# A fused attention and mixture-of-experts kernel: the routing's small tables and one product move from SBUF to PSUM

## The chip, the cores and the metric

The kernel runs on one core of a Trainium2 chip. The metric is device time in microseconds of one execution. A time is the median of several runs; beside it stands one execution recorded by the hardware profiler, from which every row below is taken.

The core has TensorE (PE, matrix products into PSUM; PEld is its weight load), VectorE (DVE), ScalarE (ACT), GpSimd (POOL) and SyncE (SP, which here issues DMAs). [...]

## What is computed

The reference has three stages: a causal attention with a cumulative bias, a mixture of eight experts with a capacity of 288 tokens each, and a gated feed-forward layer. Cut to the two stages that the change is in:

```
logits = x @ w_gate                      # x: attention's output, 2304 tokens x 512
order = argsort(-logits.flatten())       # greedy: best (token, expert) pairs first
for idx in order:
    tok, e = idx // 8, idx % 8
    if assigned[tok] >= 0 or counts[e] >= 288: continue
    assigned[tok] = e; counts[e] += 1
for e in range(8):
    mask = assigned == e
    out[mask] = relu(x[mask] @ w1[e]) @ w2[e]        # first layer, 1024 wide
h = out @ w_in                           # second layer, 2048 wide
g = h * tanh(softplus(h))
return g @ w_out
```

All data are float32 at the interface, some weights of the second layer arrive as 64-bit floats.

## The kernel before

Attention runs first (0 to about 295 us) and leaves x in DRAM and the gate's logits in `L`, 128 partitions x 18 x 8. Then `experts` handles one expert at a time; each takes the 288 tokens of its set through both layers.

**Products in three parts.** Every float32 operand of a large product is split into a high and a low part, and `mm3` (L446) issues three matmuls, high by high (L448), high by low (L449), low by high (L450). ScalarE writes the high part, then VectorE or GpSimd the low part as a difference. The splits of the first layer's weights are on ScalarE (L417) and GpSimd (L418, two SBUF inputs, 128x512), in four rotating buffers `wt`; those of the second layer's weights, done once, on ScalarE (L83) and GpSimd (L84), after three integer steps on VectorE (L101, L104, L107) that turn 64-bit floats into 32-bit ones. The function `conv` inserts these steps one at a time between other work from the first routing until the end of expert 0.

**`up(e)`** is the first layer: for each of 8 slices m a group of 12 matmuls into a bank `hp` (pool `ps_h`, three banks), `act` from it (ScalarE L507, VectorE L508), and one slice later 12 matmuls from `act` into four banks `y`. **`down(e)`** is the second: for each of 16 slices f a group of 12 matmuls into an `hp` bank, `mish` on it, and three slices later (LAG) 12 matmuls `y` from the result.

**`mish(f, p, gs)`** computes the activation of bank `p`. VectorE copies `min(p, 20)` to an SBUF buffer `a` (printed as `c`, L541), ScalarE applies four functions to `a` in place (L542 to L545), then `product` (L548, VectorE) multiplies `a - 0.5` by `p` into `a`, ScalarE writes the high part from `a` (L550), and `low` (L554, VectorE) the low part from `a` and the high part. `product` is issued four ticks after `mish` and `low` one tick later; the matmuls of a slice contain four ticks. L548 is the last reader of the bank `p`.

**`route(e)`** finds the tokens of the next expert that is to be handled. It is a generator that yields how many steps of the main work are to be issued before it goes on. Expert 0's routing runs alone with the conversion (the first routing, 295 to 350 us); the routing for expert e+1 is issued in pieces between the matmuls of `up(e)` and `down(e)`. It computes each token's best logit `m` and its expert `oh` (L246, L248), then makes six searches for a threshold. `search` (L251) compares `m` with T candidates (`mask`, L253, 128 x 18 x T; T is 64 in the first two searches, 32 in the others), counts by 18 small matmuls (L258), flags (L262), spreads the result by a diagonal matrix `diag` (L264) and a matmul (L266), and reduces it to `J` (L269). Between searches, L278 to L308 make the next candidates (`k2`, `x2`, `th2`, `b2`, `cx`, `th`, `field`). After that L310 to L357 pick the expert and count places, L360 builds one-hot slots in three instructions, and L365 to L372 the token indices, with which GpSimd gathers rows (L377). The last routing (for expert 7) has no search. The small results lie in SBUF; the matmuls of the routing write a bank of `ps_r`, a new tile each time (`rbank`, L238).

**Order.** The instructions of an engine run in the order in which the Python code issues them; an instruction that waits holds up all that are behind it on its engine. VectorE's queue thus mixes the routing, L508, L541, L548 and L554, and, until the end of expert 0, the conversion.

Of the kernel before, what the change touches and what calls it, by code (L numbers as in the profile page):

```python
# [23 lines left out]
CAP = N // E  # L24
# [3 lines left out]
def fb(ap):  # L28
    return ap.bitcast(F32)
# [181 lines left out]
def experts(ctx, tc, K, ring, ident, L, x_dram, w1, w2, cv, out):  # L211
# [26 lines left out]
    def rbank():  # L238
        return ps_r.tile([128, 512], F32, name="rt")

    def small(shape, dt, name, bufs=2):
        return rot.tile(shape, dt, name=name, bufs=bufs)

    def route(e):
        m = small([128, NT], F32, "m")
# [5 lines left out]
        def search(th, T, lead):  # L251
# [4 lines left out]
            p = rbank()  # L256
# [7 lines left out]
            nc.vector.tensor_scalar(diag[:E], ident[:E, :E], n, None, op0=OP.mult)  # L264
# [3 lines left out]
            J = small([128, 1], F32, "J")  # L268
# [6 lines left out]
        else:  # L275
# [3 lines left out]
            k2 = small([128, 64], I32, "k2", 1)  # L279
# [6 lines left out]
            b2 = small([128, 1], I32, "b2")  # L286
# [5 lines left out]
            for T, step, jr in steps:  # L292
                th = small([128, 32], I32, "th", 1)
                if field is None:
                    nc.vector.tensor_copy(th[:, :T], jr)
                else:
                    nc.vector.tensor_scalar(th[:, :T], jr, field, None, op0=OP.add)
                nc.vector.tensor_tensor(th[:, :T], th[:, :T], cx.to_broadcast([128, T]), op=OP.bitwise_xor)
                yield from search(th[:, :T], T, 6 if side["up"] else 8)
                nf = small([128, 1], F32, "field")  # L300
                if field is None:
                    nc.vector.tensor_scalar(nf, R["J"], step, None, op0=OP.mult)
                else:
                    nc.vector.scalar_tensor_tensor(nf, R["J"], step, field, op0=OP.mult, op1=OP.add)
                field = nf
            li = small([128, 1], I32, "li")
            nc.vector.tensor_copy(li, field)
            nc.vector.tensor_tensor(li, li, cx, op=OP.bitwise_xor)  # L308
            lam = fb(li)
        ge = small([128, NT], BF16, "ge")  # L310
# [4 lines left out]
        p = rbank()  # L315
        nc.tensor.matmul(p[:, 0:8 * NT], onesF, geoh.rearrange("p c e -> p (c e)"), start=True, stop=True)
        yield 4
        cnt = small([128, E], F32, "cnt")
# [4 lines left out]
        se = small([128, E], F32, "se")  # L323
# [11 lines left out]
        nc.vector.tensor_sub(g2[:, NT:], sel, fb(g2)[:, 0:NT])  # L335
        yield 8
        p = rbank()
# [6 lines left out]
        sl = small([128, 2 * NT], F32, "sl", 1)  # L344
        nc.vector.tensor_add(sl, p[:, 64:64 + 2 * NT], cb)
        nc.vector.scalar_tensor_tensor(sl, fb(g2), -4096.0, sl, op0=OP.mult, op1=OP.add)
        slf = small([128, NT], F32, "slf")
        nc.vector.tensor_tensor(slf, sl[:, 0:NT], sl[:, NT:], op=OP.min)
        jg = small([128, NT, 2], F32, "jg", 1)
        for j in range(2):  # L350
            nc.vector.tensor_scalar(jg[:, :, j], slf, JW * (j + 1) - 0.5, None, op0=OP.is_ge)
        sr = small([128, NT], F32, "sr", 1)
        nc.vector.scalar_tensor_tensor(sr, jg[:, :, 0], -float(JW), slf, op0=OP.mult, op1=OP.add)
        nc.vector.scalar_tensor_tensor(sr, jg[:, :, 1], -float(JW), sr, op0=OP.mult, op1=OP.add)
# [8 lines left out]
        p = rbank()  # L363
# [5 lines left out]
        idf = small([128, NJ + 1], F32, "idf")  # L369
        nc.vector.memset(idf[:JW, NJ:], 0.0)  # L370
        nc.vector.tensor_reduce(idf[:JW, 0:NJ], p[:JW, 0:2 * NJ].rearrange("p (j k) -> p j k", k=2), axis=AX.X, op=OP.add)
        nc.vector.tensor_sub(idx[:JW], idf[:JW, 0:NJ], idf[:JW, 1:])  # L372
# [8 lines left out]
        if e + 1 < E:  # L381
            pt = small([128, NT], F32, "pt")
            nc.vector.tensor_scalar(pt, slf, CAP - 0.5, NEG, op0=OP.is_lt, op1=OP.mult)
            pe = small([128, E], F32, "pe")
# [153 lines left out]
    def mish(f, p, gs):  # L538
# [8 lines left out]
        def product():  # L547
            nc.vector.scalar_tensor_tensor(a, a, 0.5, p[:, :CAP], op0=OP.subtract, op1=OP.mult)  # L548
            g = ring("act", [128, 2, CAP], F32R)
            nc.scalar.activation(g[:, 0], a, AF.Copy, scale=-2.0)  # L550
            later(1, low, g)

        def low(g):
            nc.vector.scalar_tensor_tensor(g[:, 1], a, -2.0, fb(g)[:, 0], op0=OP.mult, op1=OP.subtract)  # L554
            gs[f] = g
# [575 lines left out]
```

## Time and profile before

| | us |
|---|---|
| median of 3 runs | 1113.09 (1109.98 to 1115.66) |
| the profiled execution, as timed | 1109.15 |
| its span, first to last instruction | 1107.4 |
| TensorE busy | 977.1 (88%) |
| VectorE busy | 751.0 (68%) |
| ScalarE busy | 631.4 (57%) |
| GpSimd busy | 442.5 (40%) |
| mean granted clock of TensorE | 0.933 of full speed |

The profile's page gives the busy time of each engine, the groups of instructions, and the chain of work that ended last. A query of the trace lists instructions in order of time, groups them by line and shape, gives for a line the shortest, median and longest duration, lists which engine waited for which, or gives busy times and the granted TensorE clock of a stretch. "L253" is line 253 of the kernel, and `mask<-m,th` names output and inputs of an instruction; `c` is the buffer `a` of `mish`, `rt` the bank of the routing.

### The profile page before, as it was taken

What the parts mean: (1) busy time and instruction counts of PE and PEld (TensorE: products, weight loads), DVE (VectorE), ACT (ScalarE), POOL (GpSimd) and SP (SyncE); (2) the same over time, 40 slices, a digit from 0 to 9 for tenths busy, and PEclk for the clock granted to TensorE, in tenths of its full rate; (3) what the DMA queues carried; (4) which work ended last, traced back from release to release, by engine and by line L of the source; (5) the groups of instructions that cost most, each with busy time, mean ns of one, the idle gap of its engine ahead of it and who ended that gap; (6) DMA issues with size and microseconds to landing.
All of it is one profiled execution on the core that took longest, in us unless ns stands there. A gap on an engine that the chain in (4) does not pass through costs nothing.

```text
span 1107.4 us, 21467 instructions
## 1 busy us (share of the span) xinstructions
PE 977.1 (88%) x7625; PEld 932.6 (84%) x7625; DVE 751.0 (68%) x2024; ACT 631.4 (57%) x1405; POOL 442.5 (40%) x441
## 2 busy tenths in 40 slices
PE   6899999999514799979989997997998899899996
PEld 5788888888513788879979997997998899899996
DVE  7768788887797889766566656656666575744243
ACT  5567775777622356626735652762574466376574
POOL 5555665666575623450241043026025103700601
PEclk8889997999855899999999999998999999999998
DMA  5898899782325424230330121123023012500300
GB/s 131 180 212 190 196 208 202 184 193 61 99 77 164 143 68 126 78 90 1 98 98 2 55 87 56 39 60 98 2 82 97 19 39 77 150 21 13 97 1 22
DMA packets 134579, 105.58 MB, mean 95 GB/s; under 512 B 63976, under 2 KB 114312, under 8 KB 134440
## 3 DMA queue, kind: packets, MB, share of 16 engines
q1 hardware_dynamic: 122520, 83.50, 30.5%
q10 hardware_dynamic: 8880, 11.27, 3.4%
q0 software_dynamic: 3072, 9.44, 2.7%
q8 instruction: 60, 0.98, 0.4%
q14 instruction: 47, 0.39, 0.1%
HBM read 69.55 MB, written 9.73 MB: 72 GB/s over the span
## 4 chain that ended last, share of the span: by engine, by line
PE 53%; DVE 23%; issue 11%; DMA 4%; POOL 4%; ACT 4%; SPq 1%; ACTq 0%; POOLq 0%; DVEq 0%
PE hp L448 7%; PE y L449 7%; PE y L448 6%; PE y L450 6%; PE hp L450 6%; PE hp L449 6%; DVE mask L253 4%; PE pv L969 2%; POOL wt L418 2%; PE rt L258 2%; PE pv L971 1%; PE t L863 1%; PE s L931 1%; PE pv L970 1%; DMA qkraw<-in_k_dram 1%
## 5 line engine op out<-in xcount | busy, mean ns | idle before, releaser
L418 POOL TENSOR_TENSOR wt<-raw,wt 128x512 fp32r<-128x512 f32 x128 | 166.1, 1312 | 399.7 <-ACT wt L417 386.4
L948 POOL TENSOR_TENSOR Pl<-P,Ph 128x384 fp32r<-128x384 f32 (+2 forms) x128 | 137.0, 1077 | 98.0 <-DVE Ph L947 44.0
L448 PE MATMUL hp<-xu,WI 128*128 128x288 f32 x512 | 153.5, 300 | 6.2 <-DVE c L548 6.2
L448 PE MATMUL y<-act,WO 128*128 128x288 f32 x512 | 156.5, 306 | 0.0
L449 PE MATMUL y<-act,WO 128*128 128x288 f32 x512 | 152.2, 297 | 1.7 <-DVE act L554 1.5
L450 PE MATMUL y<-act,WO 128*128 128x288 f32 x512 | 151.9, 297 | 0.0
L450 PE MATMUL hp<-xu,WI 128*128 128x288 f32 x512 | 151.7, 296 | 0.0
L449 PE MATMUL hp<-xu,WI 128*128 128x288 f32 x512 | 149.9, 293 | 0.9 <-DVE xu L526 0.9
L417 ACT ACTIVATE wt<-raw 128x512 fp32r<-128x512 f32 x128 | 79.6, 624 | 74.5 <-PE y L450 41.1
L548 DVE SCALAR_TENSOR_TENSOR c<-c,hp 128x288 f32<-128x288 f32 x128 | 57.8, 452 | 81.3 <-ACT c L545 81.3
L449 PE MATMUL y<-act,wt 128*128 128x288 f32 x256 | 81.0, 316 | 27.3 <-DVE act L508 27.3
L448 PEld LDWEIGHTS hp<-xu,WI 128*128 128x128 f32 x512 | 96.4, 188 | 7.8 <-DVE c L548 7.8
L449 PEld LDWEIGHTS y<-act,WO 128*128 128x128 f32 x512 | 97.0, 189 | 2.3 <-DVE act L554 2.3
L449 PEld LDWEIGHTS hp<-xu,WI 128*128 128x128 f32 x512 | 96.9, 189 | 1.4 <-DVE xu L526 1.3
L450 PEld LDWEIGHTS y<-act,WO 128*128 128x128 f32 x512 | 97.6, 191 | 0.0
L448 PEld LDWEIGHTS y<-act,WO 128*128 128x128 f32 x512 | 97.0, 189 | 0.2 <-ACT act L550 0.2
L450 PEld LDWEIGHTS hp<-xu,WI 128*128 128x128 f32 x512 | 96.4, 188 | 0.0
L541 DVE TENSOR_SCALAR c<-hp 128x288 f32<-128x288 f32 x128 | 58.4, 456 | 48.3 <-PE hp L450 37.4
L508 DVE SCALAR_TENSOR_TENSOR act<-hp,act 128x288 fp32r<-128x288 f32 x64 | 28.6, 452 | 91.1 <-ACT act L507 91.1
L550 ACT ACTIVATE act<-c 128x288 fp32r<-128x288 f32 x128 | 56.5, 442 | 55.6 <-DVE c L548 52.0
L940 ACT ACTIVATE P<-s 128x384 f32<-128x384 f32 (+2 forms) x128 | 63.9, 504 | 41.2 <-PE s L933 21.6
L542 ACT ACTIVATE c<-c 128x288 f32<-128x288 f32 x128 | 56.6, 442 | 50.8 <-DVE c L541 48.8
(226 smaller groups left out, 2912.1 us busy)
## 6 DMA issues: line engine op xcount, KB each, us to landing
raw<-in_moe_w_dram SPq DMA_DIRECT2D x128, 256.0 KB
QKB<-qk SPq DMA_DIRECT2D x55, 288.0 KB
QKA<-qk SPq DMA_DIRECT2D x29, 288.0 KB
r<-in_moe_w_out_dram ACTq DMA_DIRECT2D x22, 256.0 KB
r<-in_moe_w_in_dram ACTq DMA_DIRECT2D x21, 256.0 KB
qkraw<-in_q_dram SPq DMA_DIRECT2D x32, 128.0 KB
qkraw<-in_k_dram SPq DMA_DIRECT2D x32, 128.0 KB
vraw<-in_v_dram SPq DMA_DIRECT2D x32, 128.0 KB
```

The costliest lines, as they stand in the source:

```text
L253: nc.vector.tensor_tensor(mask[:, :, :T], mb.to_broadcast([128, NT, T]), fb(th)[:, None, :].to_broadcast([128, NT, T]), op=OP.is_ge)
L417: nc.scalar.activation(t[:, 0], r, AF.Copy)
L418: nc.gpsimd.tensor_sub(t[:, 1], r, fb(t)[:, 0])
L448: nc.tensor.matmul(out_ap, ah, bh, start=first, stop=False)
L449: nc.tensor.matmul(out_ap, ah, bl, start=False, stop=False)
L450: nc.tensor.matmul(out_ap, al, bh, start=False, stop=last)
L541: nc.vector.tensor_scalar(a, p[:, :CAP], 20.0, None, op0=OP.min)
L542: nc.scalar.activation(a, a, AF.Exp)
L548: nc.vector.scalar_tensor_tensor(a, a, 0.5, p[:, :CAP], op0=OP.subtract, op1=OP.mult)
L550: nc.scalar.activation(g[:, 0], a, AF.Copy, scale=-2.0)
L940: nc.scalar.activation(P[:, :n], p[:, :n], AF.Exp, scale=0.125)
L948: nc.gpsimd.tensor_sub(Pl[:, :n], P[:, :n], fb(Ph)[:, :n])
```

## The change

Four kinds of edits. First, the routing has one PSUM tile `bank` for its whole life in place of a new tile for each product. Its first 144 columns take the products as before; the rest holds the routing's small tables, each at a fixed place (`inbank`): `m`, `J`, `k2`, `b2`, `low`, `lp`, `ge`, `cnt`, `se`, `sl`, `jg`, `sr`, `idp`, `pt`, `pe`, and once a copy of the 8x8 identity, `identp`. Second, where both tensor inputs of a VectorE instruction were in SBUF, one of them is now such a table; where one table was both input and output, it is split in two (`s1` and `sr`, `low` and `th`, `lp` and `li`), the scaling of `sl` (L346) is two instructions in place of one, the second half of `g2` (L335) is computed from `m` and `sel`, and one copy (`idp`) is added. Third, in `mish`, `product` writes its result over the bank `p`, and ScalarE (L550) and `low` (L554) read it there, not from `a`. Fourth, `ge` is float32, not bfloat16. The shapes of the large instructions, the issue order and the number of `hp` banks are as before.

```diff
...
 
-    def rbank():
-        return ps_r.tile([128, 512], F32, name="rt")
+    bank = ps_r.tile([128, 512], F32, name="rt")
+    place = {}
+
+    def inbank(name, n):
+        if name not in place:
+            place[name] = place.get("", 144)
+            place[""] = place[name] + n
+            assert place[""] <= 512
+        return bank[:, place[name]:place[name] + n]
+
+    identp = inbank("identp", E)
+    nc.vector.tensor_copy(identp[:E], ident[:E, :E])
 
...
     def route(e):
-        m = small([128, NT], F32, "m")
+        m = inbank("m", NT)
         nc.vector.tensor_reduce(m, L, axis=AX.X, op=OP.max)
...
             yield lead
-            p = rbank()
+            p = bank
             for c in range(NT):
...
                                     accum_out=n)
-            nc.vector.tensor_scalar(diag[:E], ident[:E, :E], n, None, op0=OP.mult)
+            nc.vector.tensor_scalar(diag[:E], identp[:E], n, None, op0=OP.mult)
             yield 4
...
             yield 2
-            J = small([128, 1], F32, "J")
+            J = inbank("J", 1)
             nc.vector.tensor_reduce(J, p[:, 64:64 + E], axis=AX.X, op=OP.max)
...
             nc.vector.tensor_scalar(b1, R["J"], float(2 ** 26), -float(2 ** 31), op0=OP.mult, op1=OP.add)
-            k2 = small([128, 64], I32, "k2", 1)
+            k2 = inbank("k2", 64).bitcast(I32)
             nc.vector.tensor_scalar(k2, j20, b1, None, op0=OP.add)
...
             yield from search(th2, 64, 16)
-            b2 = small([128, 1], I32, "b2")
+            b2 = inbank("b2", 1).bitcast(I32)
             nc.vector.scalar_tensor_tensor(b2, R["J"], float(2 ** 20), b1, op0=OP.mult, op1=OP.add)
...
                 th = small([128, 32], I32, "th", 1)
+                low = inbank("low", 32).bitcast(I32)[:, :T]
                 if field is None:
-                    nc.vector.tensor_copy(th[:, :T], jr)
+                    nc.vector.tensor_copy(low, jr)
                 else:
-                    nc.vector.tensor_scalar(th[:, :T], jr, field, None, op0=OP.add)
-                nc.vector.tensor_tensor(th[:, :T], th[:, :T], cx.to_broadcast([128, T]), op=OP.bitwise_xor)
+                    nc.vector.tensor_scalar(low, jr, field, None, op0=OP.add)
+                nc.vector.tensor_tensor(th[:, :T], low, cx.to_broadcast([128, T]), op=OP.bitwise_xor)
                 yield from search(th[:, :T], T, 6 if side["up"] else 8)
...
                 field = nf
+            lp = inbank("lp", 1).bitcast(I32)
+            nc.vector.tensor_copy(lp, field)
             li = small([128, 1], I32, "li")
-            nc.vector.tensor_copy(li, field)
-            nc.vector.tensor_tensor(li, li, cx, op=OP.bitwise_xor)
+            nc.vector.tensor_tensor(li, lp, cx, op=OP.bitwise_xor)
             lam = fb(li)
-        ge = small([128, NT], BF16, "ge")
+        ge = inbank("ge", NT)
         nc.vector.tensor_scalar(ge, m, lam, None, op0=OP.is_ge)
...
         yield 6
-        p = rbank()
+        p = bank
         nc.tensor.matmul(p[:, 0:8 * NT], onesF, geoh.rearrange("p c e -> p (c e)"), start=True, stop=True)
         yield 4
-        cnt = small([128, E], F32, "cnt")
+        cnt = inbank("cnt", E)
         nc.vector.tensor_reduce(cnt, p[:, 0:8 * NT].rearrange("p (c e) -> p e c", e=E), axis=AX.X, op=OP.add)
...
         nc.vector.tensor_reduce(top, cnt, axis=AX.X, op=OP.max)
-        se = small([128, E], F32, "se")
+        se = inbank("se", E)
         nc.vector.tensor_scalar(se, cnt, top, None, op0=OP.is_equal)
...
         nc.vector.scalar_tensor_tensor(g2[:, 0:NT], m, lam, sel, op0=OP.is_gt, op1=OP.mult)
-        nc.vector.tensor_sub(g2[:, NT:], sel, fb(g2)[:, 0:NT])
+        nc.vector.scalar_tensor_tensor(g2[:, NT:], m, lam, sel, op0=OP.is_equal, op1=OP.mult)
         yield 8
-        p = rbank()
+        p = bank
         nc.tensor.matmul(p[:, 0:2 * NT], onesF, g2, start=True, stop=True)
...
         nc.vector.tensor_tensor_scan(cb[:, 1:], p[:, 0:2 * NT - 1], zero[:, 1:], 4096.0, op0=OP.add, op1=OP.add)
-        sl = small([128, 2 * NT], F32, "sl", 1)
+        sl = inbank("sl", 2 * NT)
         nc.vector.tensor_add(sl, p[:, 64:64 + 2 * NT], cb)
-        nc.vector.scalar_tensor_tensor(sl, fb(g2), -4096.0, sl, op0=OP.mult, op1=OP.add)
         slf = small([128, NT], F32, "slf")
-        nc.vector.tensor_tensor(slf, sl[:, 0:NT], sl[:, NT:], op=OP.min)
-        jg = small([128, NT, 2], F32, "jg", 1)
+        nc.vector.scalar_tensor_tensor(slf, fb(g2)[:, 0:NT], -4096.0, sl[:, 0:NT], op0=OP.mult, op1=OP.add)
+        nc.vector.scalar_tensor_tensor(sl[:, NT:], fb(g2)[:, NT:], -4096.0, sl[:, NT:], op0=OP.mult, op1=OP.add)
+        nc.vector.tensor_tensor(slf, slf, sl[:, NT:], op=OP.min)
+        jg = inbank("jg", 2 * NT).rearrange("p (c j) -> p c j", j=2)
         for j in range(2):
             nc.vector.tensor_scalar(jg[:, :, j], slf, JW * (j + 1) - 0.5, None, op0=OP.is_ge)
-        sr = small([128, NT], F32, "sr", 1)
-        nc.vector.scalar_tensor_tensor(sr, jg[:, :, 0], -float(JW), slf, op0=OP.mult, op1=OP.add)
-        nc.vector.scalar_tensor_tensor(sr, jg[:, :, 1], -float(JW), sr, op0=OP.mult, op1=OP.add)
+        s1, sr = small([128, NT], F32, "s1", 1), inbank("sr", NT)
+        nc.vector.scalar_tensor_tensor(s1, jg[:, :, 0], -float(JW), slf, op0=OP.mult, op1=OP.add)
+        nc.vector.scalar_tensor_tensor(sr, jg[:, :, 1], -float(JW), s1, op0=OP.mult, op1=OP.add)
         nc.vector.tensor_tensor(aux[:, :, 1:], aux[:, :, 0:1].to_broadcast([128, NT, 2, 2]),
...
             yield 3 if c + 6 < NT else 8
-        p = rbank()
+        p = bank
         for c in range(NT):
...
         idx = small([128, NJ], I32, "idx", 3)
-        idf = small([128, NJ + 1], F32, "idf")
+        idf, idp = small([128, NJ + 1], F32, "idf"), inbank("idp", NJ)
         nc.vector.memset(idf[:JW, NJ:], 0.0)
         nc.vector.tensor_reduce(idf[:JW, 0:NJ], p[:JW, 0:2 * NJ].rearrange("p (j k) -> p j k", k=2), axis=AX.X, op=OP.add)
-        nc.vector.tensor_sub(idx[:JW], idf[:JW, 0:NJ], idf[:JW, 1:])
+        nc.vector.tensor_copy(idp[:JW], idf[:JW, 1:])
+        nc.vector.tensor_sub(idx[:JW], idf[:JW, 0:NJ], idp[:JW])
         R[e, "idx"] = idx
...
         if e + 1 < E:
-            pt = small([128, NT], F32, "pt")
+            pt = inbank("pt", NT)
             nc.vector.tensor_scalar(pt, slf, CAP - 0.5, NEG, op0=OP.is_lt, op1=OP.mult)
-            pe = small([128, E], F32, "pe")
+            pe = inbank("pe", E)
             nc.vector.tensor_scalar(pe, se, NEG, None, op0=OP.mult)
...
         def product():
-            nc.vector.scalar_tensor_tensor(a, a, 0.5, p[:, :CAP], op0=OP.subtract, op1=OP.mult)
+            nc.vector.scalar_tensor_tensor(p[:, :CAP], a, 0.5, p[:, :CAP], op0=OP.subtract, op1=OP.mult)
             g = ring("act", [128, 2, CAP], F32R)
-            nc.scalar.activation(g[:, 0], a, AF.Copy, scale=-2.0)
+            nc.scalar.activation(g[:, 0], p[:, :CAP], AF.Copy, scale=-2.0)
             later(1, low, g)
...
         def low(g):
-            nc.vector.scalar_tensor_tensor(g[:, 1], a, -2.0, fb(g)[:, 0], op0=OP.mult, op1=OP.subtract)
+            nc.vector.scalar_tensor_tensor(g[:, 1], p[:, :CAP], -2.0, fb(g)[:, 0], op0=OP.mult, op1=OP.subtract)
             gs[f] = g
...
```

## Rows read from the trace of the kernel before

**Rows 1.** The page's first part: busy time, share and instructions of each engine.

```profile
PE 977.1 (88%) x7625; PEld 932.6 (84%) x7625; DVE 751.0 (68%) x2024; ACT 631.4 (57%) x1405; POOL 442.5 (40%) x441
```

**Rows 2.** Waits: engine line <- releaser: us in total, times, longest.

```profile
PE y L449 <- DVE act L508: 27.3, 7, 4.8
...
PE hp L448 <- DVE c L548: 6.2, 7, 1.6
```

**Rows 3.** L253 (ns min/median/max); VectorE's L360, 466 to 560 (busy us, mean ns).

```profile
L253 DVE TENSOR_TENSOR mask<-m,th x42: 757/760/6736, 295.8 to 889.9; 128x576 fp32r<-128x576 f32 x28, 128x1152 fp32r<-128x1152 f32 x14
...
L360 DVE TENSOR_TENSOR mask<-slots,sr 128x576 bf16<-128x576 f16 x3 | 2.1, 751 | 0.0
```

**Rows 4.** Timeline: start, us, engine, instruction, [idle before <- releaser]; up stages, experts 2 and 4.

```profile
559.82 1.32 DVE L248 TENSOR_TENSOR oh<-L,m 128x144 fp32r<-128x144 f32 x1
...
570.19 6.72 DVE L253 TENSOR_TENSOR mask<-m,th 128x1152 fp32r<-128x1152 f32 x1
...
570.73 4.96 POOL L418 TENSOR_TENSOR wt<-raw,wt 128x512 fp32r<-128x512 f32 x4
...
577.33 0.61 PE L449 MATMUL y<-act,wt 128*128 128x288 f32 x1 [4.78 <-DVE act L508]
...
773.97 0.27 PE L266 MATMUL rt<-diag,onesF 128*128 128x8 f32 x1 [0.81 <-DVE diag L264]
```

**Rows 5.** Stretches: PE, PEld, DVE, ACT, POOL busy us (count), granted clock, DMA, GB/s.

```profile
577.33:585.33 8.00, 8.00 (x53) 7.66 (x53) 1.38 (x5) 1.56 (x3) 1.81 (x2) 0.65 0.09 31
...
859.63:867.63 8.00, 7.19 (x55) 6.92 (x56) 2.14 (x5) 2.19 (x4) 2.82 (x3) 0.80 0.07 25
954.36:962.36 8.00, 8.00 (x60) 7.99 (x61) 5.23 (x8) 2.15 (x4) 4.86 (x4) 0.79 0.34 98
...
405.56:413.56 8.00, 8.00 (x73) 7.88 (x74) 7.11 (x21) 5.94 (x15) 1.47 (x2) 1.00 0.36 101
456.20:464.20 8.00, 8.00 (x51) 7.98 (x52) 4.29 (x10) 4.74 (x11) 0.00 (x0) 0.79 0.12 35
```

**Rows 6.** Single lines over the whole span: ns min/median/max, first and last start.

```profile
L508 DVE SCALAR_TENSOR_TENSOR act<-hp,act x64: 435/457/459, 360.8 to 1043.4; 128x288 fp32r<-128x288 f32 x64
...
L548 DVE SCALAR_TENSOR_TENSOR c<-c,hp x128: 435/454/457, 405.1 to 1094.1; 128x288 f32<-128x288 f32 x128
...
L554 DVE SCALAR_TENSOR_TENSOR act<-c,act x128: 442/458/1873, 406.1 to 1095.1; 128x288 fp32r<-128x288 f32 x128
```

**Rows 7.** Timeline, start of the down stage, experts 2 (601) and 6 (971).

```profile
601.41 0.40 PE L448 MATMUL hp<-xu,WI 128*128 128x288 f32 x1 [0.79 <-DVE c L548]
...
601.88 0.46 DVE L554 SCALAR_TENSOR_TENSOR act<-c,act 128x288 fp32r<-128x288 f32 x1 [0.16 <-ACT act L550]
...
971.40 0.33 PE L448 MATMUL hp<-xu,WI 128*128 128x288 f32 x1
...
972.93 0.46 DVE L554 SCALAR_TENSOR_TENSOR act<-c,act 128x288 fp32r<-128x288 f32 x1 [0.87 <-ACT act L550]
...
973.03 0.32 PE L448 MATMUL y<-act,WO 128*128 128x288 f32 x1
```

**Rows 8.** Timeline, up stage of expert 6 with the routing for expert 7.

```profile
946.53 5.31 DVE L346 SCALAR_TENSOR_TENSOR sl<-g,sl 128x36 f32<-128x36 f32 x1
...
954.36 0.40 PE L449 MATMUL y<-act,wt 128*128 128x288 f32 x1 [2.94 <-DVE act L508]
```

**Rows 9.** First routing: a stretch (columns as in rows 5) and a timeline row.

```profile
300.00:320.00 20.00, 2.77 (x48) 2.39 (x49) 19.27 (x36) 7.81 (x25) 20.00 (x24) 0.50 0.23 67
...
341.70 4.23 DVE L360 TENSOR_TENSOR mask<-slots,sr 128x576 bf16<-128x576 f16 x3
```

**Rows 10.** Timeline of TensorE's waits in expert 0.

```profile
370.03 0.27 PE L266 MATMUL rt<-diag,onesF 128*128 128x8 f32 x1 [2.37 <-DVE diag L264]
...
405.56 0.40 PE L448 MATMUL hp<-xu,WI 128*128 128x288 f32 x1 [1.57 <-DVE c L548]
...
456.20 0.40 PE L449 MATMUL y<-act,WO 128*128 128x288 f32 x1 [1.51 <-DVE act L554]
```

## The prediction

> **What bounds the kernel now.** I read the page's busy shares first. TensorE is at 88% of a 1107.4 us span and VectorE at 68% [rows 1], so on average VectorE has room; what matters is whether TensorE waits for it at particular places. So the second view is the list of who waited for whom. TensorE lost 27.3 us in 7 waits for `act` from L508, and 6.2 us in 7 waits at L448 for a free `hp` bank, released by L548 [rows 2]. The third view is single lines of VectorE: L253, the mask, has a median of 760 ns and a largest of 6736 [rows 3]. Its larger shape has twice the elements of the smaller, not nine times; the same instruction, then, costs very different times. The timeline of expert 2's up stage says why: the mask of 6.72 us starts at 570.19, and GpSimd runs four L418 subtractions in one piece from 570.73 to 575.69; the mask ends 1.2 us after them. L508 stands behind it in VectorE's queue, and TensorE waits 4.78 us for L508 [rows 4]. [...]
>
> Which instructions wait for GpSimd? L508 and L548 have one input in SBUF and one in PSUM: 64 and 128 executions, none over 459 ns. L554, of the same size with both inputs in SBUF, reaches 1873 [rows 6]. One SBUF input is never held up, two can be. That is the pattern the change acts on.
>
> **The change part by part.** The sum is made on the profiled execution (span 1107.4, 1109.15 as timed); the median of the runs is 1113.09, 3.9 higher, and I take the same difference off it.
>
> *The mask, experts 1 to 5.* With `m` in PSUM the 1152-element mask should take its unblocked time: the last 1.2 us of the 6.72 are that. L508 then follows in time. TensorE's wait of 4.78 goes, in five periods: 23.9. With it goes the slow clock behind it: a mean of 0.65 over 8 us loses 2.8 us, one of 0.80 loses 1.6; these are the lowest and the last of five such stretches [rows 5]. The five come to 1.7, 2.8, 1.6, 2.7 and 1.6: 10.4.
>
> *The other held instructions in these periods.* `diag` (L264, from `ident` in SBUF) is what TensorE waits for 0.81 us once per period: 4.0. `oh` (L248) takes 1.32 us where its unblocked time is near 0.3, and delays the second L508: about 0.3 per period, 1.5 [rows 4]. All but `mask`, `oh`, `k2`, `b2` and two `diag` run while GpSimd is idle and gain nothing. Experts 1 to 5 together: 39.8.
>
> *Expert 7's routing* has no search, but L346 is held 5.31 us, and TensorE waits 2.94 for the L508 behind it [rows 8], with 1.7 of slow clock (0.79 over 8 us [rows 5]) and 0.4 at `geoh`: 5.0.
>
> *The first routing (295 to 350).* TensorE has nothing else to do there, VectorE is busy 19.27 of 20 us and GpSimd 20 of 20 [rows 9], so VectorE's time is the time. From `k2` to the three L360, 19 instructions exceed their unblocked times by 8.4 us in sum; the largest part is the three L360, 4.23 against 2.1 us [rows 9, 3]. The weight conversion (L101 to L107) shares the queue, still has two SBUF inputs and still meets GpSimd's backlog, which VectorE now reaches earlier: I take 6, with 3 and 8.4 as ends.
>
> *Expert 0* is slowed by that conversion, which doesn't change; its 2.37 us wait at 370.03 for `diag` [rows 10] comes from a held L101, and stays. The 1.51 us wait at 456.20 comes from L554 with two SBUF inputs [rows 10] and goes, with its 1.7 of slow clock (0.79 [rows 5]); small waits give 0.8. Sum 4.
>
> *What is added.* One `identp` copy, and per routing a second scaling of `sl` and a copy to `idp`: 17 instructions of some 0.17 us, three of them on the path (first routing): 0.5. No row shows VectorE writing PSUM. Nearest rows: reading PSUM costs nothing against SBUF (medians of L508 457, L548 454, L554 458 [rows 6]). I take zero; the spread of these medians, 4 ns, bounds it near zero, and since a write is not a read I keep 0.03 us an instruction either way, the spread from least to most of L508, as ends: 1 us over the first routing.
> [...]
>
> *The bank that is held longer.* This is the cost. `product` now leaves its result in the `hp` bank, and `low` (L554) reads it last. There are three `hp` banks, and in the down stage the fourth hp group takes the bank of the first. Before, L548 released it; now L554 does, and behind TensorE's waiting matmul everything of TensorE queues, the y groups first. In expert 2 the fourth group starts at 601.41 after a wait of 0.79; L554 ends at 602.34 [rows 7]: 0.97 later, five times 4.9. In expert 6 it starts at 971.40 without a wait, and L554 ends at 973.39: 2.0 later, less 0.1 that the y group already waited; twice (experts 6 and 7) 3.8. Expert 0 has two such places, about 1 each: 2. Later groups are covered: a group takes 1.63 us (971.40 to 973.03), L554 ends 5.25 after its hp group's end (968.14, two groups before 971.40, to 973.39), and the next user of the bank comes five groups, 8.15 us, later. Cover 2.9 us; without it the overrun would be paid by each later hp group.
> Does the clock fall after these longer waits? After the 1.57 us wait at 405.56 it stayed at 1.00; after the 1.51 at 456.20, with other gaps shortly before it, it fell, as after the 2.94 at 954.36 [rows 5, 8, 10]. The new waits are 1.8 (experts 1 to 5) and 2.0 (6 and 7). I let it fall in the last two, 1.7 each as at 456.20: 3.4.
>
> Sum: 39.8 + 5.0 + 6 + 4 = 54.8 gained; 4.9 + 3.8 + 2 + 3.4 + 0.5 = 14.6 paid. Net 40.2, so 1069 for the profiled execution and **1073** by the median.
>
> **The rivals.**
> *The clock falls at every down stage.* 1.8 us is longer than the wait that left it up, and about as long as the one that didn't. Five falls of 1.6 to 2.8, 2.1 on average: 10 more, 1083. 20%.
> *The weights come late instead.* With the mask gone, GpSimd's four L418 are next. TensorE reached the stalled group at 572.55 (577.33 less 4.78); the last of the four ended at 575.69 [rows 4] and serves a group three later, due 4.9 us on, at 577.4 at full speed: 1.7 to spare. Three scatters sit in the same queue. If they take the spare and 1.5 more in six periods: 9, 1081. 10%.
> *More is gained.* The conversion gets VectorE's freed time without meeting GpSimd, in the first routing and expert 0, and the bank wait shrinks, as product and mask no longer collide: 1058. 10%.
> *It doesn't do what it says.* Instructions with SBUF input and PSUM output (`k2`, `low`), or a per-partition scalar in SBUF beside an SBUF tensor, have no unblocked row. If all of these and the mask still wait, only the 14.6 are left: 1128. If `k2` alone waits, the mask ends near 571.6, just in time. 5%.
> *Slower: the bank decides every period.* The place is the hp group of each f; it decides once L554 ends over 2.9 us later than now, by a slow PSUM write or ScalarE's queue. 13 later groups in 8 experts are 104 places; at 0.6 us each 62, more than the 40.2: 1135. Nothing in the rows suggests 2.9 us. 4%.
>
> **How the numbers follow.** Forecast 51%, the others as given; measurement tells about 0.5% (5.6 us) from no change. Faster takes forecast and the first three rivals, 91%, and a fraction for mixtures: 0.92; same 0.02 (mixtures of the last two); slower 0.06. The forecast's own ends: first routing -3 to +2.4, expert 0 by 3, clock by 4, PSUM writes by 2, so 1064 to 1082. The range takes in the three faster rivals: 1055 to 1090.
>
> **What would show it.** Right: L253 at 1152 elements near 1.35 us in all 14; no wait of TensorE for L508 above 1 us; the hp waits released by L554, near 1.8 us in experts 1 to 5 and 2.0 in 6 and 7; periods of 94 us fall to some 87; first routing shorter by about 6. Wrong: masks still above 2 us; waits for L418 or ACT's `wt` in up stages; granted clock at 0.5 after the fourth hp group; waits at L448 in every f.

## The result, and the profile after

The changed kernel takes 1065.34 us (median of 4 runs, 1061.81 to 1069.36) against 1111.53 (4 runs, 1109.02 to 1115.66) for the kernel before: a ratio of 0.958, with a 95% interval of 0.954 to 0.963. The forecast was 1073, with a range of 1055 to 1090. The profiled execution after is the shortest of the four (1061.81 as timed, span 1059.9).

The page's first part, and the list of waits of TensorE (engine line <- releaser: us in total, times, longest):

```profile
PE 957.4 (90%) x7625; PEld 919.4 (87%) x7625; DVE 675.5 (64%) x2041; ACT 627.7 (59%) x1405; POOL 437.1 (41%) x441
```

```profile
PE hp L462 <- DVE act L568: 14.8, 9, 2.2
PE rt L276 <- DVE diag L274: 13.9, 10, 3.1
...
PE hp L496 <- DVE act L568: 2.1, 2, 1.6
```

VectorE has 17 instructions more than in [rows 1] and is busy 75.5 us less: what it lost was time in which it stood still inside an instruction. The wait of 27.3 us for `act` [rows 2] (that line is L522 now) is gone from the list altogether. The `hp` wait went from 6.2 to 14.8 us, and its releaser is now `low` (L568, before L554), as the change makes it.

The lines of the routing and of `mish` (ns min/median/max), then the first tables of the routing in expert 2's up stage, in the timeline of VectorE and GpSimd:

```profile
L263 DVE TENSOR_TENSOR mask<-rt,th x42: 756/757/1358, 296.6 to 844.6; 128x576 fp32r<-128x576 f32 x28, 128x1152 fp32r<-128x1152 f32 x14
L274 DVE TENSOR_SCALAR diag<-rt,n x42: 212/214/215, 299.7 to 847.8; 8x8 fp32r<-8x8 f32 x42
L562 DVE SCALAR_TENSOR_TENSOR hp<-c,hp x128: 444/462/464, 395.1 to 1046.5; 128x288 f32<-128x288 f32 x128
L568 DVE SCALAR_TENSOR_TENSOR act<-hp,act x128: 440/448/459, 396.1 to 1047.5; 128x288 fp32r<-128x288 f32 x128
```

```profile
541.33 1.29 POOL L432 TENSOR_TENSOR wt<-raw,wt 128x512 fp32r<-128x512 f32 x1 [10.47 <-ACT wt L431]
541.48 0.30 DVE L258 TENSOR_TENSOR oh<-L,rt 128x144 fp32r<-128x144 f32 x1
541.70 1.35 DVE L263 TENSOR_TENSOR mask<-rt,th 128x1152 fp32r<-128x1152 f32 x1
```

L263's largest is 1358 ns where L253's was 6736 [rows 3], so none of the 14 large masks is held. In the timeline `oh` and the mask begin inside GpSimd's subtraction (L432, before L418) and run at full pace; `oh` took 1.32 us in the same place before [rows 4]. `low` has lost its tail (459 against 1873 [rows 6]). `product`, which now writes PSUM, has a median of 462 ns against 454.

The price, at the start of the down stage of experts 2 and 3, and the granted clock of the 8 us from either restart (columns as in [rows 5]):

```profile
575.59 0.40 PE L462 MATMUL hp<-xu,WI 128*128 128x288 f32 x1 [1.74 <-DVE act L568]
...
663.26 0.40 PE L462 MATMUL hp<-xu,WI 128*128 128x288 f32 x1 [1.74 <-DVE act L568]
```

```profile
575.59:583.59 8.00, 8.00 (x64) 7.89 (x65) 3.73 (x13) 4.50 (x12) 0.00 (x0) 0.79 0.00 0
663.26:671.26 8.00, 8.00 (x74) 7.95 (x75) 4.93 (x16) 5.75 (x14) 0.00 (x0) 1.00 0.00 0
```

The attention part in front of the routing is the same in all these kernels, and yet ends between 295 and 309 us from one profile to the next, so I compare stages and not spans. A stage runs from one reduction to `m` (L246, L256 after) to the next; experts 6 and 7 are taken together, to the end of the span. In us:

| | first routing | expert 0 | experts 1 to 5 | experts 6, 7 | sum |
|---|---|---|---|---|---|
| before | 66.11 | 104.51 | 469.36 | 172.20 | 812.18 |
| after | 60.42 | 98.23 | 435.23 | 169.96 | 763.84 |
| only `m` in PSUM | 64.43 | 101.08 | 431.18 | 170.89 | 767.58 |
| only the product in PSUM | 66.47 | 106.32 | 478.29 | 175.22 | 826.30 |
| tables in PSUM, product in SBUF | 60.38 | 98.16 | 427.17 | 166.30 | 752.01 |
| the same, product of slice 0 alone in SBUF | 60.38 | 97.74 | 427.86 | 167.48 | 753.46 |
| before, GpSimd only writes | 64.91 | 94.24 | 426.84 | 166.70 | 752.69 |
| after, `diag` from SBUF | 60.30 | 98.41 | 438.84 | 171.17 | 768.72 |
| before, GpSimd's run spaced | 65.32 | 105.12 | 448.40 | 173.68 | 792.52 |

Each row is of one profiled execution, and these are not all near their kernel's median; the ratios below are of all timed runs.

### The profile page after: what moved, and what is told of

It is laid out like the page before. It is cut to its first block, busy times and chain, and to the rows that moved or that the text cites. A ratio compares the mean times of both kernels' runs of the same rounds, so it can differ in the third digit from the quotient of the medians.

```text
span 1059.9 us, 21486 instructions
## 1 busy us (share of the span) xinstructions
PE 957.4 (90%) x7625; PEld 919.4 (87%) x7625; DVE 675.5 (64%) x2041; ACT 627.7 (59%) x1405; POOL 437.1 (41%) x441
## 4 chain that ended last, share of the span: by engine, by line
PE 62%; DVE 13%; issue 9%; ACT 6%; DMA 5%; POOL 3%; SPq 1%; ACTq 0%; POOLq 0%; DVEq 0%
PE y L462 8%; PE hp L462 8%; PE y L463 7%; PE y L464 7%; PE hp L463 7%; PE hp L464 7%; PE pv L983 2%; PE t L1028 2%; PE s L945 2%; DMA qkraw<-in_k_dram 2%; PE t L877 2%; POOL wt L432 2%; PE pv L985 2%; PE pv L984 1%; PE rt L268 1%
## 5 line engine op out<-in xcount | busy, mean ns | idle before, releaser
L432 POOL TENSOR_TENSOR wt<-raw,wt 128x512 fp32r<-128x512 f32 x128 | 164.2, 1299 | 368.9 <-ACT wt L431 355.3
L462 PE MATMUL hp<-xu,WI 128*128 128x288 f32 x512 | 154.5, 302 | 14.8 <-DVE act L568 14.8
L562 DVE SCALAR_TENSOR_TENSOR hp<-c,hp 128x288 f32<-128x288 f32 x128 | 58.8, 459 | 86.5 <-ACT c L559 85.1
L522 DVE SCALAR_TENSOR_TENSOR act<-hp,act 128x288 fp32r<-128x288 f32 x64 | 29.2, 456 | 101.3 <-ACT act L521 100.6
L564 ACT ACTIVATE act<-hp 128x288 fp32r<-128x288 f32 x128 | 52.3, 408 | 60.0 <-DVE hp L562 56.8
L462 PE MATMUL hp<-xu,wt 128*128 128x288 f32 x256 | 80.8, 315 | 1.4 <-ACT xu L499 1.4
```

The source lines that it names most:

```text
L432: nc.gpsimd.tensor_sub(t[:, 1], r, fb(t)[:, 0])
L462: nc.tensor.matmul(out_ap, ah, bh, start=first, stop=False)
L522: nc.vector.scalar_tensor_tensor(h[:, 1], p[:, :CAP], 0.0, fb(h)[:, 0], op0=OP.max, op1=OP.subtract)
L562: nc.vector.scalar_tensor_tensor(p[:, :CAP], a, 0.5, p[:, :CAP], op0=OP.subtract, op1=OP.mult)
L564: nc.scalar.activation(g[:, 0], p[:, :CAP], AF.Copy, scale=-2.0)
```

## The experiments

Two theories stood behind the forecast: GpSimd's run of subtractions holds the instructions of VectorE that take their tensors from SBUF, which is the gain; and the `hp` bank of the product is held longer, which is the cost. The first four runs part the two, the next two ask what exactly is held, and the last asks why it is held so long.

**One table alone.** The kernel before, with `m` and the routing's products in one fixed PSUM bank and nothing else changed.

```diff
+    bank = ps_r.tile([128, 512], F32, name="rt")
...
-        return ps_r.tile([128, 512], F32, name="rt")
+        return bank
...
-        m = small([128, NT], F32, "m")
+        m = bank[:, 200:200 + NT]
```

> The kernel before with one part of the change: the routing has one PSUM bank and only the table m lies in it; every other table and the activation's product stay in SBUF. Theory (a VectorE instruction with two SBUF inputs waits behind GpSimd's queue, one with a PSUM input does not): mask is 1.35 us in all 14 large cases and oh 0.3; TensorE's five waits of 4.78 us for L508 and the slow clock behind them go (34 us), oh gives 1.5 and the first routing and expert 0 some 3, while the waits of 0.81 for diag, expert 7's 2.94 and k2's 1.6 us stay and no hp wait grows: about 1111 - 38 = 1073 us, ratio 0.965. Rival 1 (the next held instruction in line, k2 or th2, takes the mask's place): TensorE keeps 2 to 3 us of the wait per period and the clock still falls: about 1090. Rival 2 (it is not the SBUF input that waits, but any long VectorE instruction beside GpSimd): mask stays at 6.7 us, 1111.

Measured: 1071.98 us, ratio 0.964 (0.960 to 0.969). Its mask line and two of its waits:

```profile
L255 DVE TENSOR_TENSOR mask<-rt,th x42: 757/758/1359, 310.0 to 860.9; 128x576 fp32r<-128x576 f32 x28, 128x1152 fp32r<-128x1152 f32 x14
...
PE rt L268 <- DVE diag L266: 19.5, 14, 3.5
...
PE hp L450 <- DVE c L550: 6.1, 7, 1.6
```

```profile
924.61 0.41 PE L451 MATMUL y<-act,wt 128*128 128x288 f32 x1 [3.06 <-DVE act L510]
```

One table, an operand of `oh` and the mask, brings 38.2 us in experts 1 to 5 (469.36 to 431.18); the sum had put 35.8 on these two instructions, the 39.8 less 4.0 for `diag`. The larger mask still begins during the issue of an indirect DMA with a subtraction behind it, at 570.89, and takes 1.36 us there. The two waits that belong to other tables stay: `diag` as often as before, and 3.06 us behind the scaling of `sl` in expert 6, as in [rows 8]. The `hp` wait, with the product in SBUF, is as before.

**The product alone.** The kernel before, with the three lines of `mish` changed and the routing left as it was.

```diff
-            nc.vector.scalar_tensor_tensor(a, a, 0.5, p[:, :CAP], op0=OP.subtract, op1=OP.mult)
+            nc.vector.scalar_tensor_tensor(p[:, :CAP], a, 0.5, p[:, :CAP], op0=OP.subtract, op1=OP.mult)
...
-            nc.scalar.activation(g[:, 0], a, AF.Copy, scale=-2.0)
+            nc.scalar.activation(g[:, 0], p[:, :CAP], AF.Copy, scale=-2.0)
...
-            nc.vector.scalar_tensor_tensor(g[:, 1], a, -2.0, fb(g)[:, 0], op0=OP.mult, op1=OP.subtract)
+            nc.vector.scalar_tensor_tensor(g[:, 1], p[:, :CAP], -2.0, fb(g)[:, 0], op0=OP.mult, op1=OP.subtract)
```

> The kernel before with only the other part: the activation's product is written over the hp bank and read there by ScalarE and L554. Theory: L554 is never above 0.46 us, but TensorE's wait for the hp bank at the fourth group ends with L554 and grows by 1.0 us in experts 1 to 5 and from 0 to 1.9 in 6 and 7, with 2 us in expert 0 and a slow clock behind some of these waits (0 to 10 us); expert 0 gains about 3 from L554: slower by 7 to 17, about 1120 us, ratio 1.008. Rival (the longer hold is covered, and L554's held time is what counts): faster by 3 to 8, about 1106.

Measured: 1123.43 us, ratio 1.012 (1.008 to 1.016): by itself this part makes the kernel slower.

```profile
L554 DVE SCALAR_TENSOR_TENSOR act<-hp,act x128: 441/449/459, 416.7 to 1118.1; 128x288 fp32r<-128x288 f32 x128
...
PE hp L448 <- DVE act L554: 16.1, 9, 2.6
```

`low` is no longer held, as meant, and the wait of 1.51 us for it in expert 0 [rows 10] is gone. But the `hp` wait went from 6.2 us [rows 2] to 16.1, and expert 0 came out longer too (106.32 against 104.51).

**The change without the product.** The kernel after, with those three lines of `mish` put back to `a`.

```diff
-            nc.vector.scalar_tensor_tensor(p[:, :CAP], a, 0.5, p[:, :CAP], op0=OP.subtract, op1=OP.mult)
+            nc.vector.scalar_tensor_tensor(a, a, 0.5, p[:, :CAP], op0=OP.subtract, op1=OP.mult)
...
```

> The changed kernel with the activation's product back in the SBUF buffer, the routing's tables still in PSUM. Theory: the nine waits for the hp bank (14.8 us in sum) shrink to some 6 and are released by the product instruction again, and the slow clock after two of them goes (about 3.4); expert 0 pays some 3 for L554 with two SBUF inputs: about 9 faster than the changed kernel, 1056 us, ratio to the kernel before 0.950. Rival (L554's held time counts more than the bank): slower than the changed kernel by 3 or more, 1068.

Measured: 1051.78 us, ratio 0.949 (0.946 to 0.953), faster than both kernels. TensorE's `hp` wait falls back to what it was:

```profile
PE hp L462 <- DVE c L562: 5.2, 6, 1.1
```

Against the kernel after, experts 1 to 5 gain 8.06 us, experts 6 and 7 gain 3.66, expert 0 nothing (98.16 and 98.23), the first routing nothing. That is the price of the longer hold, by place, but for 0.65 us in expert 2: there TensorE waits 0.49 us for `diag` in the kernel after (559.38), behind an `act` (L522) that ScalarE released late. Against the run with `m` alone, the other tables are worth 4.0 us in experts 1 to 5 (431.18 to 427.17), five times the 0.81 of `diag` [rows 4], and 4.6 in experts 6 and 7.

**The product in SBUF for one slice of sixteen.** If the price is paid at the fourth `hp` group alone, which takes the bank of slice 0, then it is enough to keep slice 0's product in SBUF.

```diff
+            q = a if f == 0 else p[:, :CAP]
-            nc.vector.scalar_tensor_tensor(p[:, :CAP], a, 0.5, p[:, :CAP], op0=OP.subtract, op1=OP.mult)
+            nc.vector.scalar_tensor_tensor(q, a, 0.5, p[:, :CAP], op0=OP.subtract, op1=OP.mult)
...
-            later(1, low, g)
+            later(1, low, g, q)
```

> The changed kernel with the product in SBUF for the first slice (f = 0) of each down stage only, in PSUM for the other 15. Theory: only the fourth hp group lacks cover, so the bank of the first slice is all that has to be released early: the nine waits shrink as in the kernel with the product undone, and expert 0 keeps L554 unheld: about 11 to 12 faster than the changed kernel, 1053 us, ratio 0.948. Rival (the waits move to the fifth hp group, whose bank is now the one released late): the waits keep their 14.8 us in sum, 1065.

Measured: 1051.30 us, ratio 0.948 (0.944 to 0.951), not told apart from the run before this one. The other 15 slices hold their banks as long as in the kernel after and cost next to nothing: in experts 6 and 7 a wait moves to the next `hp` group (0.34 and 0.33 us, released by `low`), and these two take 1.18 us more than with the whole product in SBUF. The rest is covered, as the forecast's 2.9 us of cover said.

**GpSimd that only writes.** The kernel before, with L418 a fill in place of a subtraction.

```diff
-        nc.gpsimd.tensor_sub(t[:, 1], r, fb(t)[:, 0])
+        nc.gpsimd.memset(fb(t)[:, 1], 0.0)
```

> The kernel before, all tables and the product in SBUF, with one line changed: GpSimd writes zeros into the low part of the first layer's weights (L418) in place of subtracting two SBUF tensors. The weights' low part is left out of the result; the matmuls that use it are still issued. It asks whether it is GpSimd's reading of SBUF that holds VectorE's instructions with two SBUF inputs. Theory (its reading): the 14 masks of 1152 elements take about 1.36 us, TensorE's waits for L508 in experts 1 to 5 go, L554 stays under 0.5 us after expert 0, and the stages of experts 1 to 5 are 85.4 to 86.4 us as in the kernel after (93.4 to 94.5 before); about 1070 us, a ratio near 0.963. Rival (any GpSimd instruction holds them, writing too): the masks that meet the four fills still take over 2 us, by as much as the fills last, and where a fill is as long as the subtraction was (1.24 us) the waits stay at 4.8 us and the time near 1111.

Measured: 1057.28 us, ratio 0.952 (0.947 to 0.957). A fill takes 0.53 us where the subtraction took 1.29 (medians), so GpSimd is less in the way by its shorter time as well, and the time alone decides nothing. The rows where a fill lies beside a mask do (timeline, experts 5 and 1; GpSimd's work beside `k2` is in the second list):

```profile
822.17 0.76 DVE L253 TENSOR_TENSOR mask<-m,th 128x576 fp32r<-128x576 f32 x1
822.26 0.53 POOL L418 MEMSET wt<- 128x512 f32 x1 [1.16 <-PE y L448]
```

```profile
463.33 0.93 POOL L618 DMA_INDIRECT out_dram<-r,idx  x1 [0.86 <-DVE r L616]
463.57 0.68 DVE L280 TENSOR_SCALAR k<-j,b 128x64 int32<-128x64 f32 x1
464.25 1.17 POOL L418 MEMSET wt<- 128x512 f32 x2
465.15 1.36 DVE L253 TENSOR_TENSOR mask<-m,th 128x1152 fp32r<-128x1152 f32 x1
```

The mask with both inputs in SBUF takes 0.76 us, its unblocked time, with the whole fill inside it. That mask began before the fill, so the larger one says more: a fill was running when it began and had 0.27 us to go, and it takes its 1.36 us, so in all five periods. So it was GpSimd's reading that held the mask with two SBUF inputs for 6.72 us [rows 4], not its writing. `k2` (L280), with one SBUF tensor and an SBUF output, is of another kind: it takes 0.68 us, against 0.25 at its shortest, beside GpSimd's issue of an indirect DMA, and ends with it.

**`diag` put back.** The kernel after, with the identity read from SBUF again.

```diff
-            nc.vector.tensor_scalar(diag[:E], identp[:E], n, None, op0=OP.mult)
+            nc.vector.tensor_scalar(diag[:E], ident[:E, :E], n, None, op0=OP.mult)
```

> The kernel after with one operand put back: diag (L274) reads the 8x8 identity from SBUF, not from PSUM. This instruction has one SBUF tensor, a per-partition scalar in SBUF and an SBUF output. Theory (it was held by GpSimd with one SBUF tensor as well, which is what the forecast's 4.0 us for diag took): TensorE's wait of about 0.8 us for diag comes back once in each of experts 1 to 5, whose stages are 0.8 us longer each, 435.2 to about 439 in sum; with a little more in the first routing, about 1070 us, a ratio near 0.962. Rival (diag was late in the kernel before because it stood behind another held instruction): the stages stay at 435.2 within 1 us and the ratio near 0.958.

Measured: 1073.62 us, ratio 0.967 (0.963 to 0.971). Its timeline in expert 5:

```profile
824.12 2.63 POOL L432 TENSOR_TENSOR wt<-raw,wt 128x512 fp32r<-128x512 f32 x2 [0.72 <-ACT wt L431]
824.18 1.23 DVE L274 TENSOR_SCALAR diag<-ident,n 8x8 fp32r<-8x8 f32 x1
...
825.47 0.27 PE L276 MATMUL rt<-diag,onesF 128*128 128x8 f32 x1 [0.79 <-DVE diag L274]
```

Sixty-four elements take 1.23 us, held by the first of two subtractions, and TensorE waits 0.79. The wait comes back in four of the five periods, 0.79 us each, and not in expert 2, where it was expected too. Experts 1 and 3, at full clock in both profiles, are 1.05 and 1.01 us longer. The sum over experts 1 to 5, 3.61 more (438.84), is near the 4.0 by chance: the clock fell behind the bank wait in experts 2 and 5 here and in 2 and 4 in the profile after. The ratio has moved by 0.009 rather than the 0.004 of four such periods; the rest isn't explained by them, and this profile has one stretch of slower clock in experts 6 and 7 that the profile after doesn't have (171.17 against 169.96).

**The run spaced out.** The kernel before, with four fills of one element behind each subtraction.

```diff
         nc.gpsimd.tensor_sub(t[:, 1], r, fb(t)[:, 0])
+        for _ in range(4):
+            nc.gpsimd.memset(spacer, 0.0)
```

> The kernel before, with four fills of one element issued on GpSimd behind each subtraction of L418 (some 0.09 us each, as L617 takes), so that the run of four subtractions has gaps. It asks why the mask waits for all four and not for the one that is running. Theory (a mask that finds GpSimd reading goes on in the first gap): it waits for one subtraction, so 2.0 to 2.7 us in place of 6.72; TensorE's waits for L508 in experts 1 to 5 go from 4.8 to under 1 us, and their stages from 93.4 to 94.5 down to 87 to 88.5 us; ratio near 0.97. Rival (the mask waits until GpSimd has no further subtraction queued, gaps or not): the four now last 6.3 us with the fills between them, the mask takes about 8 us, the waits grow to about 6 us, stages of 95 to 96, ratio near 1.01.

Measured: 1091.22 us, ratio 0.985 (0.979 to 0.990). Expert 2's timeline, up stage:

```profile
566.55 1.93 DVE L282 TENSOR_SCALAR x<-k 128x64 int32<-128x64 int32 x1
567.11 1.30 POOL L418 TENSOR_TENSOR wt<-raw,wt 128x512 fp32r<-128x512 f32 x1
...
568.77 1.36 DVE L253 TENSOR_TENSOR mask<-m,th 128x1152 fp32r<-128x1152 f32 x1
...
570.95 1.27 POOL L418 TENSOR_TENSOR wt<-raw,wt 128x512 fp32r<-128x512 f32 x1
...
572.28 0.40 PE L452 MATMUL y<-act,wt 128*128 128x288 f32 x1 [1.32 <-POOL spacer L420]
```

Stages of 89.3 to 91.1 us in experts 1 to 5 lie between the two expectations, and the run answers its question only in part. The fills shifted GpSimd's work in time, the run of four no longer formed beside the mask, and no large mask met a subtraction in experts 1 to 5; for the mask itself it is left open whether a gap would let it go on. A smaller instruction with one SBUF tensor, L324, shows it for its kind (`se`, expert 6; rows of this run, then of the kernel before):

```profile
920.16 1.88 DVE L324 TENSOR_SCALAR se<-cnt,top 128x8 f32<-128x8 f32 x1
920.70 1.29 POOL L418 TENSOR_TENSOR wt<-raw,wt 128x512 fp32r<-128x512 f32 x1
```

```profile
939.15 3.12 DVE L324 TENSOR_SCALAR se<-cnt,top 128x8 f32<-128x8 f32 x1
939.67 2.55 POOL L418 TENSOR_TENSOR wt<-raw,wt 128x512 fp32r<-128x512 f32 x2
```

Both times L324 began while GpSimd was issuing an indirect DMA. Before, it was held through the two subtractions behind the issue; with fills behind the first, it was held through that one alone. `x2` (L282) in the list above, begun in an issue too, is likewise held to the end of the one subtraction behind it. A mask that begins beside the fills is not held (expert 5):

```profile
850.94 0.76 DVE L253 TENSOR_TENSOR mask<-m,th 128x576 fp32r<-128x576 f32 x1
851.32 1.50 POOL L418 TENSOR_TENSOR wt<-raw,wt 128x512 fp32r<-128x512 f32 x1
```

It is the next subtraction that then takes 1.50 us, 0.21 more than its 1.29. The run also shows another price, that of the rival in which the weights come late: GpSimd is later with its part of them, and TensorE waits 1.3 us for it in each of experts 1 to 6 and 1.6 in expert 7.

## Why the prediction was right, and by how much its terms were off

The chain of reasons held. The mask, its hold by GpSimd's run and the wait behind it were read rightly, and the cost was expected at the right instruction. TensorE has no wait for `act` or for weights above 0.25 us in experts 1 to 7 any more, so the rival of the late weights did not come. The net was forecast at 40.2 us for the profiled execution; the stages give 48.3 (812.18 to 763.84). By part:

| | forecast | measured |
|---|---|---|
| experts 1 to 5: tables | 39.8 | 42.2 (before to product in SBUF) |
| experts 1 to 5: bank | -4.9 | -8.1 |
| experts 6, 7: tables | 5.0 | 5.9 |
| experts 6, 7: bank and clock | -3.8 and -3.4 | -3.7 |
| expert 0, net | 4 - 2 | 6.3 |
| first routing, net | 6 - 0.5 | 5.7 |

*Experts 1 to 5, gain.* 42.2 against 39.8. The run with `m` alone parts it as the sum did: 38.2 for the mask and `oh`, 4.0 for the other tables, where the sum had 4.0 for `diag`; with `diag` put back, a period in which its wait returns costs some 1.0.

*The bank.* The waits are those that were announced: 1.81, 1.74, 1.74, 1.75 and 1.75 us in experts 1 to 5 (forecast 1.8), 1.83 and 1.84 in 6 and 7 (forecast 2.0). What was mis-sized is the clock behind them, in both places. The forecast let it stay up in experts 1 to 5 and fall in 6 and 7. In the profiled execution it fell to a mean of 0.79 in experts 2 and 4 (stages of 88.39 and 87.68 against 86.36 to 86.43 in the others) and in none of the last two. So five holds of 0.95 are 4.8 us, as forecast; the two falls cost 1.3 each, as expert 4 shows, and the later `diag` in expert 2 makes up the 8.1. The rival in which the clock falls at every down stage came in two of five. That 2.6 us of clock stand in experts 2 and 4 where 3.4 were forecast in 6 and 7 brings the sum near by luck.

*Where the clock falls.* The step that took one wait of 1.57 us without a fall and one of 1.51 with it, and from there let the clock fall in the last two periods alone, had no ground. The rows above are two waits of 1.74 us at the same place of two periods, one with a mean of 0.79 behind it and one with 1.00. In the run with the product alone the mean after the same wait was 0.79 in experts 1 and 5 (1.80 and 1.73 us) and 1.00 in experts 2 to 4 (1.73); in the run with `diag` put back it was 0.79 in experts 2, 5 and 7 (1.74, 1.74 and 1.83) and 1.00 in the others. Between these the length of the wait does not decide. What does is left open; the four timed executions after have mean clocks of 0.948, 0.941, 0.941 and 0.946, the highest in the shortest.

*Expert 0.* This is the step that failed: "its 2.37 us wait at 370.03 for `diag` comes from a held L101, and stays". The same place before and after (timeline; rows of before first):

```profile
361.66 1.34 DVE L248 TENSOR_TENSOR oh<-L,m 128x144 fp32r<-128x144 f32 x1
...
368.01 1.36 DVE L101 TENSOR_SCALAR c<-r 128x256 int32<-128x256 int32 x1
```

```profile
356.82 0.30 DVE L258 TENSOR_TENSOR oh<-L,rt 128x144 fp32r<-128x144 f32 x1
...
363.01 0.62 DVE L101 TENSOR_SCALAR c<-r 128x256 int32<-128x256 int32 x1
...
364.06 0.27 PE L276 MATMUL rt<-diag,onesF 128*128 128x8 f32 x1 [0.31 <-DVE diag L274]
```

L101 is unchanged, and takes 0.33 us more than its median of 0.29 where it took 1.07 more. `oh`, nine instructions in front of it, is 1.04 us shorter, and the GpSimd subtraction that holds L101 begins 5.70 us after the reduction to `m` where it began 6.62 after it. L101 itself begins 6.53 us after the reduction, against 6.68, since the `act` in front of it waits for ScalarE. So it meets the end of the subtraction and not its start. The matmul behind `diag` starts 7.58 us after the reduction in place of 8.70. How long this unchanged instruction was held, 1.07 or 0.33 us, depended on when it arrived; I took it as a property of the instruction. The granted clock in the 8 us from there stayed at 1.00 in place of 0.79. The tables alone bring 6.35 us here (104.51 to 98.16), `m` alone 3.4 of it. In the other step, that the held L554 goes for 3.2 and the bank costs 2, the wait for L554 did go, and so did the slow clock behind it. But with the tables in PSUM and the product in SBUF that wait was 1.29 us with no slow clock, and the bank's longer waits took it back: 2.16 us against 1.08 in the down stage, and 0.51 and 1.59 against 0.47 at its end (L496). So expert 0 takes 98.23 us with the product in PSUM and 98.16 without.

*First routing.* 5.7 us against 5.5. The routing's own instructions run at their unblocked times (`oh` takes 303 to 305 ns in all 8 routings and `diag` 212 to 215 in all 42 searches), and the conversion gives some of it back, as the choice of 6 between 3 and 8.4 had it: L107's largest in this stage went from 943 to 4458 ns, beside GpSimd's issue of a gather and the four subtractions behind it.

*What the median adds.* 7.7 us separate forecast and median. The profiled execution came out at 1061.8 against 1069; the median lies 3.5 above it, near the 3.9 that the forecast took.

*A slip and an open working.* The rival of the late weights adds 9 us to 1073, which is 1082 and not 1081. How the ends 1064 and 1082 come from the listed spreads (3, 3, 4 and 2 one way, 2.4, 3, 4 and 2 the other) is not shown; added up they give 1062 and 1085. Neither bears on the result.

*Writing PSUM.* Zero was taken, with 0.03 us either way: `product` takes 462 ns against 454 [rows 6]. `low`, which now reads PSUM, takes 448 ns against 458 from SBUF. The forecast's ends count 2 us for PSUM writes, where its 0.03 us an instruction comes to 1 us over the first routing; no run shows the 2 us. What the runs show is 8 ns more for `product`, at the median, and 0.04 us more for each `k2` than its shortest before.

## What to carry over

When one shape of a line has a largest time far above its median, look at what the neighbouring engine ran in that stretch before costing the line itself: here one table moved from SBUF to PSUM was worth 38 of the 48 us. A PSUM bank is not free memory: every result left in it keeps the bank until its last reader is done, and with the three banks here that showed where the pipeline starts up (waits of 14.8 us in place of 6.2), so move tables that nobody queues for and leave the product where it was. After any such move, expect the unchanged instructions to be held at other places than before, as L101 was here for 0.33 us in place of 1.07, and forecast their sum with a margin instead of carrying single waits over.

## What the runs showed of the hardware that I had not expected

- **Three kinds of VectorE instructions.** With one tensor in PSUM (the mask, `oh`, `low`, `k2` and `diag` after) no row shows them held by GpSimd: their longest take 1.36, 0.31, 0.46, 0.29 and 0.22 us. With two inputs in SBUF the mask was held by GpSimd's reading (6.72 us [rows 4]), not by its writing (1.36 us beside a fill). With one SBUF tensor and an SBUF output (`k2`, `x2`, `diag` from `ident`, L101) they were held as well: by subtractions (1.23 us for 64 elements), by a fill (0.57 us for `x2` at 464.28 in the run with fills, 0.20 at its shortest) and by the issue of an indirect DMA (0.68 us for `k2`, though it took 0.25 where it began 0.11 us into an issue, at 566.26 in the run with gaps). The forecast's sentence that one SBUF input is never held up came from lines that also read PSUM (459 and 457 ns at most [rows 6]), and fails for these; a reduction from SBUF to SBUF was not held (L322 before, 0.16 us inside a subtraction at 336.37).
- **A whole run, or one instruction.** The mask of 6.72 us [rows 4] began while GpSimd was issuing a scatter, whose row is below, 0.54 us before the first subtraction; the run of four followed at 570.73 without a gap, and the mask ended 1.2 us after the last. It is so in all five periods. The issue alone did not hold L284: with two SBUF inputs too, it began and ended inside it at 569.93 and took its shortest 0.22 us. What GpSimd does when an instruction begins parts most cases in the trace before. L324 (two subtractions, 3.12 us) and L346 (four, 5.31 us) began in an issue as well. But 41 held instructions (0.1 us or more above their shortest) began during a subtraction with another right behind it, and 39 of them waited for the first alone. A mask at 302.00, in the rows below, is one: the next subtraction then took 1.84 us in place of 0.72. So is `diag` put back, which waited for the first of two (824.18 to 825.41, the run lasting to 826.75). There are exceptions (L554 waited for two at 454.28; in the run with the product alone a mask was let go after three of four, 487.72), and why an issue makes the difference is open. A mask that began beside fills and before a subtraction was not held (0.76 us at 850.94).

```profile
569.78 0.93 POOL L618 DMA_INDIRECT out_dram<-r,idx  x1 [0.17 <-DVE k L280]
```

```profile
302.00 1.78 DVE L253 TENSOR_TENSOR mask<-m,th 128x1152 fp32r<-128x1152 f32 x1
...
302.53 1.84 POOL L84 TENSOR_TENSOR WO<-xu,WO 128x256 fp32r<-128x256 f32 x1
```

- **The cost of the other output.** `k2` written to PSUM takes 0.29 us at every one of its 7 executions, against 0.25 at its shortest before and 1.59 at its median.
